# Attention into a feed-forward pair on one core: where the last softmax sums, scalings and roundings are put

## The chip, the cores and the metric

One core of one Trainium2 chip. The metric is device time in microseconds of one execution, the median of several. The kernel before: 574.27 us (three runs, 572.66 to 574.66).

## What is computed

Attention with capped scores (2 batches, 12 heads, 448 positions, head size 64), its output x (896 x 768) through two feed-forward layers, all in float32:

```python
scores = cap * np.tanh(q @ k.T / np.sqrt(64) / cap)
attn = np.exp(scores - max) ; attn /= attn.sum(-1) + 1e-09
x = (attn @ v) laid out as (2 * 448, 12 * 64)
x = (s * relu(x @ w_in) ** 2 + b) @ w_out        # 768 -> 2048 -> 768
h = x @ w2_in
out = (h * clip(h + 3, 0, 6) / 6) @ w2_out       # 768 -> 2048 -> 768
```

## The kernel before

All matrices are held transposed: channels on partitions, 448 positions of one batch on the free axis.

**Attention** goes over 12 pairs of heads (`P = 12`; pairs 0 to 5 are batch 0, pairs 6 to 11 batch 1). A pair's 448 keys are three chunks of 128 and a rest of 64; the rests of two neighbouring pairs form one mixed unit, so two pairs make 7 units (`U = 7`, `N = 42` in all). A unit goes through `scores` (PE, L221 and L225, into PSUM tile `ps`), `tanh` and `exps` (ACT, L229 and L234, tile `t`), `attend` (PE, L244 and L247, adding into the pair's PSUM tile `pav`) and `add_up` (DVE, L256 and L259, adding the exponentials into `acc`). The order is written out by hand: one loop over steps `n` (L358) emits each engine's work, `attend` and `scores` for two units at each even step, and a table `plan` adds the rest at given steps.

The softmax sums of two pairs are made by PE with a matrix of ones: `total` (L266, over `acc`) and `total_rest` (L274, over the mixed unit) write PSUM tile `pz`, of which there is one buffer (`ps_z`, one bank). DVE takes the reciprocal (L276, into `rz`), and DMAs on SP's queue write it to DRAM (L280) and read it back spread over partitions (L282, tile `rb`). `take` (DVE, L300) copies a pair's `pav` to SBUF as `xu`; `finish_x` (DVE) multiplies it by `rb` (L306) and splits it into a rounded part `xh` (L307) and the remainder `xl` (L308). The last two pairs, 10 and 11, do without DRAM: `total_pair` (PE, L289 and L292, also into `pz`; reciprocal L295) gives sums that are already spread.

**The feed-forward part** (`ffn`) works from weights in chunks of 128 x 768. They come as 64-bit numbers and are joined and split in stages: `fetch` (DMA, tile `raw`), `rescale` (DVE L66 or ACT L68), `join` (DVE L80, L82, L84), `upper` (the rounded part `whi`, DVE or ACT, L93), `lower` (the remainder `wlo`, DVE L99). Each product takes three matmuls, `wlo` by `xh`, `whi` by `xl`, `whi` by `xh` (L104). It opens with the first three chunks (`FIRST = 3`, made ready during attention by the table `early`) against batch 0, 54 matmuls into three PSUM tiles `pf`, then against batch 1, 54 more. `pf` has four buffers, which take the banks of `ps` once attention's scores are done. Matmuls of batch 0 (nine a step) begin at step `N - 1 = 41`, between the last steps of attention; those of batch 1 read pair 6's x first and pair 11's last. After batch 0 come the ReLUs (ACT, L110), squares (L114) and `gh`, `gl` (L121, L128), and beside batch 1 chunk 3 is joined and split.

The steps that matter at the end are these:

```python
for d in range(P // 2 - 1):
    at_step(U * d + 11, total, d)
    at_step(U * d + 12, total_rest, d)
    for o in range(2):
        at_step(U * d + 17 + o, finish_x, 2 * d + o)
for p in range(P):
    at_step(U * (p // 2) + 6 + 3 * (p % 2), take, p)
at_step(N - 1, total_pair, P - 2)
at_step(N + 1, finish_x, P - 2)
at_step(N + 2, total_pair, P - 1)
at_step(N + 4, finish_x, P - 1)
```

Of the kernel before, what the change touches and what calls it, by code (L numbers as in the profile page):

```python
# [7 lines left out]
F32 = mybir.dt.float32  # L8
# [7 lines left out]
B, H, S, D = 2, 12, 448, 64  # L16
# [13 lines left out]
def attention_moe_moe(ctx: ExitStack, tc: tile.TileContext, qk, v, cap, w1i, w1o, s, b, w2i, w2o, out):  # L30
    nc = tc.nc
# [12 lines left out]
    x = [[act.tile([128, KD, S], F32R, name=f"x{p}{bi}") for p in ("h", "l")] for bi in range(B)]  # L44
# [9 lines left out]
    def fetch(i):  # L54
        if i < len(chunks):
            src, k0, k1 = chunks[i]
            raws[i] = wp.tile([128, CH * 128, 2], U32, name="raw", tag="raw")
            nc.sync.dma_start(raws[i][:, :(k1 - k0) * 128, :], src[:, k0:k1, :].bitcast(U32).rearrange("p k (m t) -> p (k m) t", t=2))
# [102 lines left out]
    def psum():  # L161
        return ps_f.tile([128, 512], F32, name="pf")
# [28 lines left out]
    at = tc.alloc_tile_pool(name="at", bufs=3)  # L191
    dram = ctx.enter_context(tc.tile_pool(name="dram", bufs=2, space=bass.MemoryType.DRAM))
    ps_v = tc.alloc_tile_pool(name="ps_v", bufs=3, space=PSUM)
    ps_z = tc.alloc_tile_pool(name="ps_z", bufs=1, space=PSUM)
    ps_s = tc.alloc_tile_pool(name="ps_s", bufs=2, space=PSUM)
    P = B * H // 2
    units = [u for d in range(P // 2) for u in [(2 * d, c) for c in range(NC)] + [(2 * d, None)] + [(2 * d + 1, c) for c in range(NC)]]
    N, U = len(units), 2 * NC + 1
    raw_qk, u_ps, u_t, acc, mix, pav, xu, sums, rz, rb = {}, {}, {}, {}, {}, {}, {}, {}, {}, {}
# [5 lines left out]
    def load(p):  # L205
        bi, hp = divmod(p, H // 2)
        raw_qk[p] = at.tile([128, 2, S], F32, name="rqk", bufs=4)
        if p == 0:
            nc.scalar.dma_start(raw_qk[p][:, 1, :], qk[bi, hp, :, 1, :])
            nc.sync.dma_start(raw_qk[p][:, 0, :], qk[bi, hp, :, 0, :])  # L210
        else:
            nc.sync.dma_start(raw_qk[p], qk[bi, hp])

    def scores(n):

        p, c = units[n]
        ps = u_ps[n] = ps_s.tile([128, 2, 512], F32, name="ps")
        for j in range(2):
            rows = (top, end)[j]
            if c is not None:  # L220
                nc.tensor.matmul(ps[:, j, :S], raw_qk[p][rows, 1, c * 128:(c + 1) * 128], raw_qk[p][rows, 0, :], start=True, stop=True)  # L221
        if c is None:
            for o, j, keys, col in MIXED:
                rows = (top, end)[j]
                nc.tensor.matmul(ps[keys, col, :S], raw_qk[p + o][rows, 1, NC * 128:], raw_qk[p + o][rows, 0, :], start=True, stop=True)  # L225

    def tanh(n):
        u_t[n] = at.tile([128, 2, S], F32, name="t", bufs=8)
        nc.scalar.activation(u_t[n], u_ps.pop(n)[:, :, :S], AF.Tanh, scale=icap_r)  # L229

    def exps(n):


        nc.scalar.activation(u_t[n], u_t[n], AF.Exp, scale=cap_r)  # L234

    def attend(n):
        p, c = units[n]
        bi, d = divmod(p // 2, H // 4)
        new = p + 1 if c is None else p if c == 0 and p % 2 == 0 else None
        if new is not None:  # L240
            pav[new] = ps_v.tile([128, 512], F32, name="pav")
        if c is None:
            for o, j, keys, col in MIXED:
                nc.tensor.matmul(pav[p + o][(top, end)[j], :S], va[bi][keys, d, 4 * NC + col, :], u_t[n][keys, col, :], start=o == 1, stop=o == 0)  # L244
            return
        for j in range(2):
            nc.tensor.matmul(pav[p][(top, end)[j], :S], va[bi][:, d, (2 * (p % 2) + j) * NC + c, :], u_t[n][:, j, :],  # L247
                             start=(p % 2 == 0 and c == 0), stop=(p % 2 == 1 and c == NC - 1))
# [35 lines left out]

    def total_pair(p):

        z = ps_z.tile([128, 512], F32, name="pz")
        for j in range(2):
            nc.tensor.matmul(z[(top, end)[j], :S], ones, acc[p][:, j, :], start=True, stop=False)  # L289
        for o, j, keys, col in MIXED:  # L290
            if o == p % 2:
                nc.tensor.matmul(z[(top, end)[j], :S], ones[keys, :], mix[p // 2][keys, col, :], start=False, stop=True)  # L292
        del acc[p]
        rb[p] = at.tile([128, S], F32, name="rz", bufs=2)
        nc.vector.reciprocal(rb[p], z[:, :S])  # L295

    def take(p):

        xu[p] = at.tile([128, S], F32, name="xu", bufs=6)
        nc.vector.tensor_copy(xu[p], pav.pop(p)[:, :S])  # L300

    def finish_x(p):
        bi, hp = divmod(p, H // 2)
        hi, lo = (t[:, hp, :] for t in x[bi])
        xf = xu.pop(p)
        nc.vector.tensor_mul(xf, xf, rb.pop(p))  # L306
        nc.vector.tensor_copy(hi, xf)  # L307
        nc.vector.tensor_sub(lo, xf, hi.bitcast(F32))  # L308

    with tc.manual_schedule():  # L310
        nc.scalar.dma_start(capt, cap)
        load(0)
        nc.sync.dma_start(va[0][:, 0], v[0][:, 0])
        load(1)
        load(2)
        nc.sync.dma_start(va[0][:, 1:], v[0][:, 1:])
        load(3)
        for i in range(3):
            fetch(i)
        nc.sync.dma_start(st, s.to_broadcast([128, 1]))  # L320
        nc.sync.dma_start(bt, b.to_broadcast([128, 1]))
        nc.sync.dma_start(va[1], v[1])
        nc.vector.memset(zeros, 0.0)
        nc.gpsimd.memset(ones, 1.0)
        nc.scalar.activation(three, zeros[:, :1], AF.Tanh)
        warm = ps_z.tile([128, 512], F32, name="pz")
        for columns in WARM:
            nc.tensor.matmul(warm[:, :columns], zeros[:, :128], zeros[:, :columns], start=True, stop=True)
        nc.vector.reciprocal(icap, capt)
        nc.vector.tensor_scalar(icap, icap, SCALE, None, op0=ALU.mult)  # L330
        cap_r, icap_r = (nc.scalar.alloc_register(n) for n in ("cap_r", "icap_r"))
        nc.scalar.reg_load(cap_r, capt.bitcast(I32))
        nc.scalar.reg_load(icap_r, icap.bitcast(I32))
        nc.vector.memset(three, 3.0)
        early = {}
        for i in range(FIRST):
            for j, step in enumerate(((rescale, i, True), (join, i, 0), (join, i, 1), (join, i, 2), (upper, i, True), (lower, i))):
                early[6 + 6 * i + j] = [step]
        early[38] = [(rescale, FIRST)]

        plan = {}
        at_step = lambda n, what, *args: plan.setdefault(n, []).append((what, args))
        for d in range(P // 2 - 1):
            at_step(U * d + 11, total, d)
            at_step(U * d + 12, total_rest, d)
            for o in range(2):
                at_step(U * d + 17 + o, finish_x, 2 * d + o)
        for p in range(P):
            at_step(U * (p // 2) + 6 + 3 * (p % 2), take, p)
        at_step(N - 1, total_pair, P - 2)  # L350
        at_step(N + 1, finish_x, P - 2)
        at_step(N + 2, total_pair, P - 1)
        at_step(N + 4, finish_x, P - 1)
        for p in range(4, P):
            at_step(U * (p // 2 - 2) + 2 + 3 * (p % 2), load, p)
        fill, ps_f = None, None
        has = lambda n: 0 <= n < N
        for n in range(-2, N + 5):  # L358
            if n % 2 == 0 and has(n - 1):
                attend(n - 2)  # L360
                attend(n - 1)
            if n % 2 == 0 and has(n + 2):
                scores(n + 2)
                scores(n + 3)
            if n == N - 1:
                ps_s.release()
                ps_f = tc.alloc_tile_pool(name="ps_f", bufs=4, space=PSUM)
                fill = ffn()
            if n >= N - 1:
                for _ in range(3):  # L370
                    next(fill)
            if has(n):
                exps(n)
            if has(n + 1):
                tanh(n + 1)
            if n % 2 == 0 and has(n - 1):
                add_up(n - 2)
                add_up(n - 1)
            for what, args in plan.get(n, ()):
                what(*args)  # L380
            for step, *args in early.get(n, ()):
                step(*args)
        at.release()
        gp = ctx.enter_context(tc.tile_pool(name="gp", bufs=1))
        for f in range(KF):
            for bi in range(B):
                if (bi, f) not in g:
                    g[bi, f] = [gp.tile([128, S], F32R, name=f"g{p}{bi}{f}") for p in ("h", "l")]
        for _ in fill:
            pass  # L390
        for p in (ps_f, ps_z, ps_v):
            p.release()
# [40 lines left out]
```

## Time and profile before

| | |
|---|---|
| median of three runs | 574.27 us (572.66 to 574.66) |
| profiled execution | 573.65 us, span 571.9 us (first to last instruction) |
| PE busy | 561.4 us, 98% |
| DVE busy | 381.6 us, 67% |
| ACT busy | 257.0 us, 45% |
| chain that ended last | PE 86% (L104 alone 80%), DVE 9%, DMA 3% |
| PE in the 40 slices | `8999997999999999999999999999999999999997` |
| TensorE clock in the 40 slices | `9999998999999999999999999999999999999999` |

A digit of the last two lines is the busy share, or the granted clock, of one fortieth of the span in tenths (9 is 90% or more). The seventh slice, 85.8 to 100.1 us, is where attention ends. In the rows below, a matmul of attention (float32) shows as two instructions, one of the feed-forward part as one; PE rows are read best by their starts, since the ends are modelled and overlap.

### The profile page before, as it was taken

The page shows a single profiled execution, that of the slowest core. Times are in us where ns is not written, and L with a number is a line of the kernel's source. Part 1 is how long each engine was busy: PE and PEld are TensorE (multiplying, and loading weights), DVE is VectorE, ACT ScalarE, POOL GpSimd, SP SyncE. Part 2 cuts the span into 40 slices and gives each one's busy share as a digit, 9 for nine tenths or more (in the row PEclk, how much of TensorE's full clock was granted, in tenths as well). Part 3 has the DMA queues.
Part 4 walks back from the last instruction along what each step waited for, and adds up shares of the span by engine and source line. Part 5 has one row for each costly group of instructions (what it writes and reads, how often), then busy time and mean ns, then how long its engine had stood idle before and what let it go on. Part 6 is the DMA issues. An engine that isn't in the chain of part 4 may idle for free.

```text
span 571.9 us, 6988 instructions
## 1 busy us (share of the span) xinstructions
PE 561.4 (98%) x2790; PEld 460.1 (80%) x2790; DVE 381.6 (67%) x533; ACT 257.0 (45%) x368; POOL 0.4 (0%) x5
## 2 busy tenths in 40 slices
PE   8999997999999999999999999999999999999997
PEld 3223232789999999999999999999999999999996
DVE  2659987899877778446545648888888854554420
ACT  5998892155555554222322334555555522321210
POOL 0000000000000000000000000000000000000000
PEclk9999998999999999999999999999999999999999
DMA  8713421033333324234224323323332345443100
GB/s 344 286 43 126 148 66 61 3 111 110 112 111 112 111 92 135 88 128 122 84 91 146 122 100 111 104 102 103 100 102 89 120 146 156 132 124 122 59 33 33
DMA packets 14987, 64.13 MB, mean 112 GB/s; under 512 B 2006, under 2 KB 3818, under 8 KB 14826
## 3 DMA queue, kind: packets, MB, share of 16 engines
q1 hardware_dynamic: 14808, 63.45, 33.5%
q8 instruction: 22, 0.36, 0.3%
q10 hardware_dynamic: 146, 0.23, 0.1%
q14 instruction: 11, 0.09, 0.1%
HBM read 60.88 MB, written 2.79 MB: 111 GB/s over the span
## 4 chain that ended last, share of the span: by engine, by line
PE 86%; DVE 9%; DMA 3%; issue 1%; ACT 1%; SPq 0%; ACTq 0%; DVEq 0%
PE pf L104 80%; DVE rz L276 3%; PE ps L221 2%; PE pav L247 2%; DMA rb<-rows 1%; DVE xu L306 1%; DVE xl L308 1%; DMA rqk<-in_qk 1%; DVE xh L307 1%; DVE acc L259 1%; DVE acc L256 1%; DMA rows<-rz 1%; PE pz L292 0%; DVE xu L300 0%; PE pz L289 0%
## 5 line engine op out<-in xcount | busy, mean ns | idle before, releaser
L104 PE MATMUL pf<-xl,whi 128*128 128x448 f32 x384 | 140.5, 366 | 0.3 <-DVE xl L308 0.2
L104 PE MATMUL pf<-xh,wlo 128*128 128x448 f32 x384 | 140.7, 366 | 0.0
L104 PE MATMUL pf<-gh,wlo 128*128 128x448 f32 x384 | 140.3, 365 | 0.0
L104 PE MATMUL pf<-gh,whi 128*128 128x448 f32 x384 | 140.3, 365 | 0.0
L104 PE MATMUL pf<-xh,whi 128*128 128x448 f32 x384 | 140.3, 365 | 0.0
L104 PE MATMUL pf<-gl,whi 128*128 128x448 f32 x384 | 140.3, 365 | 0.0
L93 ACT CAST whi<-w 128x768 fp32r<-128x768 f32 (+1 forms) x65 | 51.7, 796 | 166.8 <-PE pf L104 96.9
L99 DVE TENSOR_TENSOR wlo<-w,whi 128x768 fp32r<-128x768 f32 (+1 forms) x68 | 61.7, 907 | 83.7 <-ACT whi L93 83.7
L104 PEld LDWEIGHTS pf<-xh,wlo 128*128 128x128 f32 x384 | 72.2, 188 | 8.1 <-issue 1.4
L104 PEld LDWEIGHTS pf<-xl,whi 128*128 128x128 f32 x384 | 72.1, 188 | 6.6 <-DVE xl L308 0.9
L104 PEld LDWEIGHTS pf<-gh,wlo 128*128 128x128 f32 x384 | 72.2, 188 | 5.7
L104 PEld LDWEIGHTS pf<-gh,whi 128*128 128x128 f32 x384 | 72.2, 188 | 5.7
L104 PEld LDWEIGHTS pf<-xh,whi 128*128 128x128 f32 x384 | 72.2, 188 | 5.7
L104 PEld LDWEIGHTS pf<-gl,whi 128*128 128x128 f32 x384 | 72.2, 188 | 5.7
L84 DVE SCALAR_TENSOR_TENSOR w<-raw,w 128x768 uint32<-128x768 uint32 (+1 forms) x68 | 61.9, 911 | 2.3
L82 DVE SCALAR_TENSOR_TENSOR w<-raw,w 128x768 uint32<-128x768 uint32 (+1 forms) x68 | 62.0, 911 | 2.2
L68 ACT ACTIVATE raw<-raw 128x768 f32<-128x768 f32 (+1 forms) x65 | 56.2, 864 | 0.0
L229 ACT ACTIVATE t<-ps 128x896 f32<-128x896 f32 x42 | 37.9, 902 | 9.9 <-PE ps L221 9.7
L234 ACT ACTIVATE t<-t 128x896 f32<-128x896 f32 x42 | 39.9, 950 | 1.3
L110 ACT ACTIVATE h<-pf 128x448 f32<-128x448 f32 x32 | 16.9, 541 | 44.4 <-PE pf L104 44.4
L80 DVE TENSOR_SCALAR w<-raw 128x768 uint32<-128x768 uint32 (+1 forms) x68 | 35.9, 528 | 0.0
L221 PE MATMUL ps<-rqk 64*128 64x448 f32 x144 | 34.0, 578 | 0.6 <-DMA rqk<-in_qk 0.4
(50 smaller groups left out, 339.9 us busy)
## 6 DMA issues: line engine op xcount, KB each, us to landing
raw<-in_w1i SPq DMA_DIRECT2D x16, 768.0 KB, 4.4
raw<-in_w2i SPq DMA_DIRECT2D x16, 768.0 KB, 4.2
raw<-in_w1o SPq DMA_DIRECT2D x12, 768.0 KB, 4.5
raw<-in_w2o SPq DMA_DIRECT2D x12, 768.0 KB, 4.5
rqk<-in_qk SPq DMA_DIRECT2D x11, 448.0 KB, 7.1
raw<-in_w1o SPq DMA_DIRECT2D x6, 512.0 KB, 3.9
raw<-in_w2o SPq DMA_DIRECT2D x6, 512.0 KB
out<-y SPq DMA_DIRECT2D x12, 224.0 KB, 2.0
```

Source lines behind the costliest of these rows:

```text
L68: nc.scalar.activation(up, up, AF.Copy, scale=2.0**-112)
L80: nc.vector.tensor_scalar(bits, up, 3, None, op0=ALU.logical_shift_left)
L82: nc.vector.scalar_tensor_tensor(out=bits, in0=up, scalar=0x80000000, in1=bits, op0=ALU.bitwise_and, op1=ALU.bitwise_or)
L84: nc.vector.scalar_tensor_tensor(out=bits, in0=low, scalar=29, in1=bits, op0=ALU.logical_shift_right, op1=ALU.bitwise_or)
L93: (nc.vector.tensor_copy if dve else nc.scalar.copy)(ready[i][0][:, :n], whole[i][:, :n])
L99: nc.vector.tensor_sub(lo[:, :n], whole.pop(i)[:, :n], hi[:, :n].bitcast(F32))
L104: nc.tensor.matmul(ps[:, :S], w[a][:, sl], rhs[r], start=(k == 0 and i == 0), stop=(k == n_k - 1 and i == 2))
L110: nc.scalar.activation(t, ps[:, :S], AF.Relu, **({"bias": three} if layer else {}))
L221: nc.tensor.matmul(ps[:, j, :S], raw_qk[p][rows, 1, c * 128:(c + 1) * 128], raw_qk[p][rows, 0, :], start=True, stop=True)
L229: nc.scalar.activation(u_t[n], u_ps.pop(n)[:, :, :S], AF.Tanh, scale=icap_r)
L234: nc.scalar.activation(u_t[n], u_t[n], AF.Exp, scale=cap_r)
L276: nc.vector.reciprocal(rz, z[:, :S])
```

## The change

Sums: the sums of pair 10 go to a `pf` tile and one step later (step 42, behind `attend` of the last two units and nine more feed-forward matmuls); all `total` and `total_rest` are one step earlier. Scaling: pairs 10 and 11 are no longer copied by `take`; the multiplication reads `pav` in PSUM. Rounding: `finish_x` is split into `scale_x` and `rest_x`, and the rounded parts of pairs 8 to 11 are made by ACT. Weights: of the three early chunks, 1 and 2 are rescaled and rounded by ACT, and their stages lie at other steps.

```diff
     def total_pair(p):
-        z = ps_z.tile([128, 512], F32, name="pz")
+        z = psum() if p % 2 == 0 else ps_z.tile([128, 512], F32, name="pz")
...
+    def scale_x(p, engine=nc.vector.tensor_copy):
+        bi, hp = divmod(p, H // 2)
+        last = p >= P - 2
+        xf = xu[p] = at.tile([128, S], F32, name="xu", bufs=6) if last else xu[p]
+        nc.vector.tensor_mul(xf, pav.pop(p)[:, :S] if last else xf, rb.pop(p))
+        engine(x[bi][0][:, hp, :], xf)
+
+    def rest_x(p):
+        bi, hp = divmod(p, H // 2)
+        nc.vector.tensor_sub(x[bi][1][:, hp, :], xu.pop(p), x[bi][0][:, hp, :].bitcast(F32))
+
     def finish_x(p):
-        bi, hp = divmod(p, H // 2)
-        hi, lo = (t[:, hp, :] for t in x[bi])
-        xf = xu.pop(p)
-        nc.vector.tensor_mul(xf, xf, rb.pop(p))
-        nc.vector.tensor_copy(hi, xf)
-        nc.vector.tensor_sub(lo, xf, hi.bitcast(F32))
+        scale_x(p)
+        rest_x(p)
...
         for i in range(FIRST):
-            for j, step in enumerate(((rescale, i, True), (join, i, 0), (join, i, 1), (join, i, 2), (upper, i, True), (lower, i))):
-                early[6 + 6 * i + j] = [step]
+            for j, step in enumerate(((rescale, i, i == 0), (join, i, 0), (join, i, 1), (join, i, 2), (upper, i, i == 0), (lower, i))):
+                early.setdefault(((6, 7, 8, 9, 10, 11), (12, 13, 14, 15, 20, 21), (20, 21, 22, 23, 28, 29))[i][j], []).append(step)
...
         for d in range(P // 2 - 1):
-            at_step(U * d + 11, total, d)
-            at_step(U * d + 12, total_rest, d)
-            for o in range(2):
+            at_step(U * d + 10, total, d)
+            at_step(U * d + 11, total_rest, d)
+            for o in range(2 if 2 * d < P - 4 else 0):
                 at_step(U * d + 17 + o, finish_x, 2 * d + o)
-        for p in range(P):
+        for p in range(P - 2):
             at_step(U * (p // 2) + 6 + 3 * (p % 2), take, p)
-        at_step(N - 1, total_pair, P - 2)
-        at_step(N + 1, finish_x, P - 2)
+        at_step(N, total_pair, P - 2)
+        at_step(N + 2, scale_x, P - 2, nc.scalar.copy)
         at_step(N + 2, total_pair, P - 1)
-        at_step(N + 4, finish_x, P - 1)
+        at_step(N + 2, rest_x, P - 2)
+        for o in (4, 3):
+            at_step(N + 3, scale_x, P - o, nc.scalar.copy)
+        at_step(N + 4, scale_x, P - 1, nc.scalar.copy)
+        for o in (4, 3, 1):
+            at_step(N + 4, rest_x, P - o)
```

How the instructions then stand, at three places. **PE, end of attention** (names: `pz` the old tile of sums, `pf` a feed-forward tile, `pav` the attention output of a pair, `xh`/`xl` the two parts of x, `whi`/`wlo` of the weights). Before, the rows around the sums of pair 10:

```order
L104 MATMUL pf<-xl_75,whi 128x448
L104 MATMUL pf<-xh_74,whi 128x448
L289 MATMUL pz<-acc,ones 64x448 x2
L292 MATMUL pz<-t,ones 64x448 x2
L247 MATMUL pav<-t,va_99 64x448 x4
L104 MATMUL pf<-xh_74,wlo 128x448
```

With the change, from the end of the first nine feed-forward matmuls:

```order
L247 MATMUL pav<-t,va_99 64x448 x4
L104 MATMUL pf<-xh_74,wlo 128x448
L104 MATMUL pf<-xl_75,whi 128x448
L104 MATMUL pf<-xh_74,whi 128x448
L104 MATMUL pf<-xh_74,wlo 128x448
L104 MATMUL pf<-xl_75,whi 128x448
L104 MATMUL pf<-xh_74,whi 128x448
L104 MATMUL pf<-xh_74,wlo 128x448
L104 MATMUL pf<-xl_75,whi 128x448
L104 MATMUL pf<-xh_74,whi 128x448
L289 MATMUL pf<-acc,ones 64x448 x2
L292 MATMUL pf<-t,ones 64x448 x2
```

The sums of pair 10 stand behind the last `attend` and nine more matmuls, and write `pf`. **DVE, the last x** (`rz` a reciprocal, `rb` one that came back from DRAM, `xu` a pair's unrounded x). Before, from the copy of pair 11's `pav` on:

```order
L300 COPY xu<-pav 128x448
L295 RECIPROCAL rz<-pz 128x448
L306 TENSOR_TENSOR xu<-xu,rb 128x448
L307 CAST xh_76<-xu 128x448
L308 TENSOR_TENSOR xl_77<-xu,xh_76 128x448
L306 TENSOR_TENSOR xu<-xu,rb 128x448
L307 CAST xh_76<-xu 128x448
L308 TENSOR_TENSOR xl_77<-xu,xh_76 128x448
L306 TENSOR_TENSOR xu<-xu,rz 128x448
L307 CAST xh_76<-xu 128x448
L308 TENSOR_TENSOR xl_77<-xu,xh_76 128x448
```

With the change, from the reciprocal of pair 10 on:

```order
L295 RECIPROCAL rz<-pf 128x448
L306 TENSOR_TENSOR xu<-pav,rz 128x448
L295 RECIPROCAL rz<-pz 128x448
L311 TENSOR_TENSOR xl_77<-xu,xh_76 128x448
L306 TENSOR_TENSOR xu<-xu,rb 128x448 x2
L306 TENSOR_TENSOR xu<-pav,rz 128x448
L311 TENSOR_TENSOR xl_77<-xu,xh_76 128x448 x3
L114 SCALAR_TENSOR_TENSOR h<-h,st 128x448 x3
```

The casts have left DVE, and the three multiplications (pairs 8, 9, 11) stand ahead of the three remainders. **ACT, behind the last exponential.** Before:

```order
L234 ACTIVATE t<-t 128x896
L110 ACTIVATE h<-pf 128x448 x3
L68 ACTIVATE raw<-raw 128x768
L121 ACTIVATE gh_78<-h,bt 128x448
L121 ACTIVATE gh_80<-h,bt 128x448
```

With the change:

```order
L234 ACTIVATE t<-t 128x896
L307 CAST xh_76<-xu 128x448 x4
L110 ACTIVATE h<-pf 128x448 x3
L68 ACTIVATE raw<-raw 128x768
L121 ACTIVATE gh_78<-h,bt 128x448
```

The four casts stand ahead of batch 0's ReLUs.

## Rows read from the trace of the kernel before

**Rows 1.** Who waited for whom, PE: us in total, times, longest.
```profile
PE pz L289 <- DVE rz L276: 3.4, 1, 3.4
...
PE pz L266 <- DVE acc L259: 0.5, 1, 0.5
...
PE pf L104 <- DVE xl L308: 0.2, 1, 0.2
```
**Rows 2.** Timeline of PE, 82 to 124 us: start, length, instruction, count, idle before.
```profile
82.45 1.73 PE L247 MATMUL pav<-t,va 128*64 128x448 f32 x8
84.10 1.77 PE L221 MATMUL ps<-rqk 64*128 64x448 f32 x8
...
89.40 0.48 PE L104 MATMUL pf<-xh,wlo 128*128 128x448 f32 x1
...
91.15 0.37 PE L104 MATMUL pf<-xh,whi 128*128 128x448 f32 x1
94.95 1.24 PE L289 MATMUL pz<-acc,ones 128*64 128x448 f32 x4 [3.43 <-DVE rz L276]
...
100.00 0.47 PE L104 MATMUL pf<-xh,wlo 128*128 128x448 f32 x1
...
105.37 0.37 PE L104 MATMUL pf<-xh,whi 128*128 128x448 f32 x1
105.67 0.97 PE L289 MATMUL pz<-acc,ones 128*64 128x448 f32 x4
...
107.47 0.47 PE L104 MATMUL pf<-xh,wlo 128*128 128x448 f32 x1
...
111.22 0.37 PE L104 MATMUL pf<-xh,wlo 128*128 128x448 f32 x1
...
113.79 0.47 PE L104 MATMUL pf<-xl,whi 128*128 128x448 f32 x1 [0.19 <-DVE xl L308]
...
115.72 0.36 PE L104 MATMUL pf<-xh,whi 128*128 128x448 f32 x1
...
123.21 0.37 PE L104 MATMUL pf<-xh,wlo 128*128 128x448 f32 x1
```
**Rows 3.** Busy time by stretch: us, PE, PEld, DVE, ACT, POOL, granted clock, DMA.
```profile
96.00:98.00 2.00, 2.00 (x8) 0.48 (x8) 0.07 (x1) 0.00 (x0) 0.00 (x0) 0.50 0.01 4
...
100.00:102.00 2.00, 2.00 (x12) 1.87 (x11) 1.90 (x3) 0.00 (x0) 0.00 (x0) 1.00 0.12 36
```
**Rows 4.** Timeline of DVE, 79 to 122 us.
```profile
79.30 2.95 DVE L276 RECIPROCAL rz<-pz 128x448 f32<-128x448 f32 x1
...
88.69 0.63 DVE L306 TENSOR_TENSOR xu<-xu,rb 128x448 f32<-128x448 f32 x1 [1.24 <-DMA rb<-rows]
...
91.95 2.95 DVE L276 RECIPROCAL rz<-pz 128x448 f32<-128x448 f32 x1
...
107.59 2.96 DVE L295 RECIPROCAL rz<-pz 128x448 f32<-128x448 f32 x1 [2.40 <-PE pz L292]
110.46 0.56 DVE L306 TENSOR_TENSOR xu<-xu,rb 128x448 f32<-128x448 f32 x1
...
111.48 0.63 DVE L308 TENSOR_TENSOR xl<-xu,xh 128x448 fp32r<-128x448 f32 x1
112.03 0.62 DVE L306 TENSOR_TENSOR xu<-xu,rb 128x448 f32<-128x448 f32 x1
...
114.73 0.63 DVE L308 TENSOR_TENSOR xl<-xu,xh 128x448 fp32r<-128x448 f32 x1
...
121.31 0.95 DVE L99 TENSOR_TENSOR wlo<-w,whi 128x768 fp32r<-128x768 f32 x1
```
**Rows 5.** Who waited for whom, ACT, 30 to 90 us.
```profile
ACT t L229 <- PE ps L221: 5.5, 6, 1.6
```
**Rows 6.** Groups by line and shape, 125 to 570 us: busy, mean ns of one.
```profile
L68 ACT ACTIVATE raw<-raw 128x768 f32<-128x768 f32 x50 | 45.4, 907 | 0.0
L93 ACT CAST whi<-w 128x768 fp32r<-128x768 f32 x52 | 43.5, 837 | 154.6 <-PE pf L104 96.9 <-DVE w L84 57.7
...
L117 DVE TENSOR_TENSOR h<-pf,h 128x448 f32<-128x448 f32 x32 | 20.0, 625 | 1.1
...
L123 ACT CAST gh<-h 128x448 fp32r<-128x448 f32 x32 | 16.5, 567 | 0.1
```

## The prediction, made before the changed kernel's time was known

> **What bounds the kernel now.** I read the page first: PE is busy for 561.4 of 571.9 us and carries 86% of the chain that ended last, so a gain has to come out of the 10.5 us in which PE stood still, or out of work that PE did slowly. The list of PE's waits says where: the largest is 3.4 us, once, at the sums of a last pair, which wait for a reciprocal on DVE [rows 1]. The reader should see that nearly everything else on the list is tenths.
>
> Next the timeline of PE at that place [rows 2]. Nine feed-forward matmuls run from 89.40, the last starts at 91.15. Then PE stands until 94.95, when pair 10's sums start. The tile `pz` has one buffer; it still holds the sums of pairs 8 and 9, and their reciprocal runs on DVE only from 91.95 for 2.95 us [rows 4]. Behind the sums in PE's order stand the last `attend` and every further matmul, so the whole engine waits. The wait has a tail: sums and `attend` take from 94.95 to 100.00, 5.05 us, though their pieces take 1.80 (105.67 to 107.47) and 1.65 (82.45 to 84.10) elsewhere [rows 2]. [...]
>
> At the other end of this stretch, batch 1's first matmuls wait in pieces for the `xl` of the last pairs, 113.13 to 115.72 [rows 2], while DVE still splits x until 115.36 [rows 4]. From the 72nd feed-forward matmul (115.72) PE runs without a wait on the list.
>
> **Part by part, from the first feed-forward matmul (89.40) to the 72nd (115.72): 26.32 us now.**
>
> *Sums of pair 10 in `pf`.* Nothing is in the way of that tile: three `pf` tiles hold batch 0's results, this is the fourth. The work of PE in its new order is, from [rows 2]: nine matmuls, 1.75 for eight starts and 0.30 to the next group (105.37 to 105.67), 2.05; `attend` 1.65; nine more, 2.05; sums of pair 10, 1.80; 18 matmuls 3.85 (107.47 to 111.22, and 0.10 for the change of group); sums of pair 11, 1.80; 18 matmuls 3.75; 17 starts at 3.75/18, 3.54. Sum 20.49, so 26.32 holds 5.83 us too much. It splits into 3.50 of standing (91.45 to 94.95), 1.60 of half clock (5.05 less 3.45) and 0.73 of waits for `xl`. The first two go: **5.10 us**. They go even if DVE were as late as before: pair 11's sums, which still need `pz`, start at 89.40 + 2.05 + 1.65 + 2.05 + 1.80 + 3.85 = 100.80, and the reciprocal that holds it ends at 94.90 [rows 4].
>
> *What is late next: x of pairs 8 to 11.* The sums of pair 11 start at 100.80, their reciprocal 1.92 later (105.67 to 107.59 before), at 102.72. It holds DVE for 2.87 (107.59 to 110.46); then come, 0.55 apart (111.48 to 112.03), the remainder of 10, the products of 8, 9 and 11, the remainders of 8, 9 and 11 [rows 4]. The remainder of 8 starts at 105.59 + 4 x 0.55 = 107.79 and ends at 108.42. PE begins batch 1 at 100.80 + 1.80 + 3.75 = 106.35 and needs that remainder seven starts later, at 107.81. So it waits some 0.65 us, and with a restart 0.75: as much as the 0.73 before, a term of nothing. The remainders of 9 and 11 end at 108.97 and 109.52, at about or before their use.
>
> *Casts on ACT.* ACT has nothing to do there; a cast of this shape takes 0.57 us [rows 6]. Pair 8's product ends near 106.75, its cast by 107.4, before DVE comes to its remainder; pair 11's product ends at 107.87 and its cast at 108.45, before 108.89, where its remainder is due. On DVE the chain from the reciprocal of pair 11 to the last `xl` shrinks from 7.77 (107.59 to 115.36) to 6.8. No further term.
>
> *Products read from PSUM.* Two copies fall away on DVE; `pav` is held longer, but no later pair asks for it. A product with one operand in PSUM takes 625 ns (L117), from SBUF 0.62 us (L306) [rows 4, 6]: no term.
> [...]
>
> *Early chunks on ACT.* ACT gains two rescalings and two roundings, 2 x 0.91 + 2 x 0.84 = 3.5 us [rows 6], between its exponentials. Their cover is the 5.5 us, in six pieces, in which ACT waits for PE from 30 to 90 us [rows 5]. DVE is relieved by as many. Bounds: nothing lost, or all 3.5 us; I take nothing, since the added pieces lie at four steps and PE has a whole unit in stock at each, and keep a part of it for the range.
>
> *Sums one step earlier.* In front of `attend` they do the same work on PE. The 0.5 us in which the sums waited for `acc` [rows 1] may go, as DVE is less behind; against it, scores behind such a group come one group, 0.9 us, later, and ACT with them. Bounds 0.5 gained and 0.9 lost; I take nothing. On SP one fetch of weights changes place with one load of q and k; that chunk is used only in the feed-forward part. The reciprocals' DMAs keep their places among the loads.
>
> **Sum.** The profiled execution took 573.65 us: 571.9 of span and 1.75 around it. Less 5.10 that is 568.55, forecast **568.6 us**. The profiled execution lies 0.6 under the median of 574.27, within the runs' spread.
>
> **Rivals.**
>
> *ACT becomes a bound in attention.* For it: from 30 us on, PE's scores need the tanh of two units before, and the added work comes in lumps of up to 1.7 us. Against it: 5.5 us of ACT's idle time against 3.5 of work. With all of it on PE's path: 568.55 + 3.5 = 572.0, no change to speak of.
>
> *The wait moves to chunk 3.* The first matmul that needs it stands 37 starts behind the 72nd, at 123.21 before, and its `wlo` ended at 122.26 [rows 2, 4], only 1 us ahead. If that chain (ReLU, squares, joins) came no earlier, PE would win 1.0: 572.6. Against it: the chain hangs on the last `xl`: from its start, 114.73, to 122.26 are 7.53 us. With the last remainder at 108.89 it ends at 116.4; PE, 5.1 earlier, needs it at 118.1.
>
> *ReLUs behind the casts: slower.* On ACT batch 0's ReLUs now queue behind four casts, and pair 11's cast queues behind DVE's products of 8 and 9, which wait for `rb` to come back from DRAM. PE's 73rd matmul, near 110.8, writes a `pf` tile that a ReLU must have read; it should be free by 109.0 (108.45 and one ReLU). If `rb` came late, PE would stand again, and a stand as long as the old one brings the half clock: 3.5 us of it with 1.6 of clock eat the whole gain. That is the point from which it decides: the last cast 5.3 us later than worked out. To be over 0.5% slower takes 2.9 more: some 577. For it: DVE did wait for `rb` at 88.69. Against it: that was 6.4 us behind the end of its reciprocal (82.25); even from 94.90, as late as before, `rb` would be there at 101.3, and it is first needed at 106.1 [rows 4].
>
> **How the numbers follow.** A measurement of this kernel can tell about 0.5% (2.9 us) from no change, so faster means under 571.4. The forecast has 0.87, ACT as a bound 0.06, chunk 3 0.04 (both no change), the ReLUs 0.03. Range: downwards both waits that I left in (0.5 and 0.7) give 567.4, and the runs spread by some tenths more: 567.0. Upwards the 0.9 of the earlier sums, part of ACT's 3.5 and the spread: 571.0.
>
> **What would show it.** Right: PE's wait at L289 for L276 is gone, the granted clock stays at 1.00 from 86 to 102 us, the stretch from the first to the 72nd feed-forward matmul takes about 21.2 us, and the first of them still starts near 89.4. The steps are wrong, each by itself, if the first L104 starts after 90.5 (ACT), if the wait for `xl` exceeds 1.5 us, if PE waits for `wlo` of chunk 3 or for a ReLU, or if PE waits at L289 for anything. A time above 571.4 would make the prediction wrong.

## The result, and the profile after

The changed kernel took 567.23 and 567.28 us, where the kernel before takes 574.27: ratio 0.9885, 95% interval 0.9842 to 0.9928. That is 7.0 us less; the forecast was 5.7 less (568.6 us), with a range from 567.0 to 571.0. Two more executions of it took 576.31 and 578.0 us; single ones of the kernel before (583.2 to 583.5 us) and of e5, e7 and e10 below also took about 9 us more, and the comparisons leave those out.

The profiled execution took 567.23 us with a span of 565.4, so the span lost 6.5 us (571.9 before). The page's first part and the start of its fourth:

```profile
PE 558.6 (99%) x2790; PEld 459.2 (81%) x2790; DVE 376.8 (67%) x523; ACT 261.1 (46%) x376; POOL 0.4 (0%) x5
...
PE 94%; ACT 3%; issue 1%; DMA 1%; DVE 0%; ACTq 0%
```

DVE stood in 9% of the chain that ended last, and is now out of it. Who PE waited for, the whole list:

```profile
PE pz L335 <- DVE zeros L330: 1.4, 1, 1.4
PE ps L225 <- ACT t L229: 0.8, 1, 0.8
PE ps L221 <- ACT t L229: 0.4, 2, 0.3
PE ps L221 <- DMA rqk<-in_qk: 0.3, 1, 0.3
PE pf L104 <- DVE xl L311: 0.3, 1, 0.3
```

Of [rows 1] the wait of 3.4 us (L289 for L276) and the one of 0.5 us (L266 for `acc`) are gone; the wait for `xl` stands at 0.3. PE at the end of attention, as in [rows 2]:

```profile
88.21 0.47 PE L104 MATMUL pf<-xh,wlo 128*128 128x448 f32 x1
...
90.23 1.72 PE L247 MATMUL pav<-t,va 128*64 128x448 f32 x8
...
93.90 0.97 PE L289 MATMUL pf<-acc,ones 128*64 128x448 f32 x4
...
95.70 0.47 PE L104 MATMUL pf<-xh,wlo 128*128 128x448 f32 x1
...
99.60 0.97 PE L289 MATMUL pz<-acc,ones 128*64 128x448 f32 x4
...
105.22 0.37 PE L104 MATMUL pf<-xh,wlo 128*128 128x448 f32 x1
...
107.14 0.47 PE L104 MATMUL pf<-xl,whi 128*128 128x448 f32 x1 [0.32 <-DVE xl L311]
...
109.27 0.36 PE L104 MATMUL pf<-xh,whi 128*128 128x448 f32 x1
```

Both groups of sums start without a wait, and from the first feed-forward matmul (88.21) to the 72nd (109.27) are 21.06 us, for 26.32 before. The view by stretches, columns as in [rows 3], shows a granted clock of 1.00 where it had been 0.50:

```profile
96.00:98.00 2.00, 2.00 (x11) 1.83 (x10) 2.00 (x1) 0.00 (x0) 0.00 (x0) 1.00 0.00 0
```

DVE in the same stretch, as in [rows 4]: it now waits for PE ahead of both reciprocals of the last pairs; ahead of the first of these sums PE used to wait for DVE.

```profile
87.15 2.95 DVE L276 RECIPROCAL rz<-pz 128x448 f32<-128x448 f32 x1
...
95.82 2.96 DVE L295 RECIPROCAL rz<-pf 128x448 f32<-128x448 f32 x1 [3.57 <-PE pf L292]
...
101.52 2.96 DVE L295 RECIPROCAL rz<-pz 128x448 f32<-128x448 f32 x1 [2.09 <-PE pz L292]
...
106.47 1.69 DVE L311 TENSOR_TENSOR xl<-xu,xh 128x448 fp32r<-128x448 f32 x3
...
114.12 0.95 DVE L99 TENSOR_TENSOR wlo<-w,whi 128x768 fp32r<-128x768 f32 x1
```

So 5.26 us of the 6.5 come from where the forecast put them. The other 1.2 lie ahead of it: the first feed-forward matmul starts at 88.21 in place of 89.40, which the forecast held unchanged. To find them the span is cut at three starts that every trace shows: the scores of a mixed unit near 51 us (L225), the first and the 72nd feed-forward matmul. The kernels e1, e2 and so on are those of the next section.

| profiled execution of | to L225 | to 1st L104 | to 72nd L104 | to the end | span |
|---|---|---|---|---|---|
| before | 51.42 | 37.98 | 26.32 | 456.2 | 571.9 |
| the change | 50.85 | 37.36 | 21.06 | 456.1 | 565.4 |
| e1_tile_back | 50.85 | 37.36 | 21.06 | 456.1 | 565.4 |
| e2_tile_only | 51.29 | 37.98 | 21.28 | 456.2 | 566.7 |
| e3_place_only | 51.70 | 37.98 | 21.55 | 456.2 | 567.4 |
| e4_early_back | 51.04 | 36.52 | 21.10 | 456.1 | 564.8 |
| e5_sums_late | 50.85 | 36.51 | 21.11 | 456.1 | 564.6 |
| e6_dve_casts | 51.62 | 37.35 | 22.35 | 456.2 | 567.5 |
| e7_early_spread | 51.06 | 36.52 | 21.10 | 465.1 | 573.8 |
| e9_best | 50.89 | 36.52 | 20.52 | 465.1 | 573.0 |
| e10_wait_back | 51.16 | 36.51 | 21.26 | 456.2 | 565.1 |
| e11_wait_short | 51.63 | 36.51 | 20.72 | 456.1 | 565.0 |
| e12_after_no_wait | 50.82 | 37.35 | 20.51 | 465.1 | 573.8 |

The first column differs by up to 0.8 us between kernels whose programs are the same up to there (the change shows 50.85 and e6, which differs in the last casts alone, 51.62). The 0.57 us between the kernel before and the change are of that kind: the first scores of a mixed unit start at 10.12 us before and at 9.53 with the change, ahead of everything that was changed, and from there to the ones near 51 us are 41.30 and 41.32. The second and third columns repeat to some hundredths wherever the program does; so does the fourth, but for the 9 us more of e7, e9 and e12, of which more below.

### The profile page after: what moved, and what is told of

It is laid out like the page before. It is cut to its first block, busy times and chain, and to the rows that moved or that the text cites. A ratio compares the mean times of both kernels' runs of the same rounds, so it can differ in the third digit from the quotient of the medians.

```text
span 565.4 us, 6987 instructions
## 1 busy us (share of the span) xinstructions
PE 558.6 (99%) x2790; PEld 459.2 (81%) x2790; DVE 376.8 (67%) x523; ACT 261.1 (46%) x376; POOL 0.4 (0%) x5
## 4 chain that ended last, share of the span: by engine, by line
PE 94%; ACT 3%; issue 1%; DMA 1%; DVE 0%; ACTq 0%
PE pf L104 82%; PE ps L221 5%; PE pav L247 4%; ACT t L229 2%; PE pav L244 1%; ACT t L234 1%; PE pz L266 1%; DMA rqk<-in_qk 1%; PE ps L225 1%; PE pz L274 1%; DVE xu L306 0%; DVE xl L311 0%; PE pz L292 0%; PE pf L289 0%; PE pz L289 0%
## 5 line engine op out<-in xcount | busy, mean ns | idle before, releaser
L104 PE MATMUL pf<-xh,wlo 128*128 128x448 f32 x384 | 140.7, 366 | 0.0
L104 PE MATMUL pf<-xl,whi 128*128 128x448 f32 x384 | 140.4, 366 | 0.3 <-DVE xl L311 0.3
L104 PE MATMUL pf<-xh,whi 128*128 128x448 f32 x384 | 140.3, 365 | 0.0
L104 PE MATMUL pf<-gl,whi 128*128 128x448 f32 x384 | 140.2, 365 | 0.0
L104 PE MATMUL pf<-gh,whi 128*128 128x448 f32 x384 | 140.2, 365 | 0.0
L104 PE MATMUL pf<-gh,wlo 128*128 128x448 f32 x384 | 140.2, 365 | 0.0
L93 ACT CAST whi<-w 128x768 fp32r<-128x768 f32 (+1 forms) x67 | 53.4, 797 | 166.3 <-PE pf L104 96.9
L99 DVE TENSOR_TENSOR wlo<-w,whi 128x768 fp32r<-128x768 f32 (+1 forms) x68 | 61.7, 907 | 83.7 <-ACT whi L93 83.7
L104 PEld LDWEIGHTS pf<-xh,wlo 128*128 128x128 f32 x384 | 72.1, 188 | 8.5 <-issue 2.1
L104 PEld LDWEIGHTS pf<-xl,whi 128*128 128x128 f32 x384 | 72.1, 188 | 6.4 <-DVE xl L311 0.7
L104 PEld LDWEIGHTS pf<-xh,whi 128*128 128x128 f32 x384 | 72.1, 188 | 5.7
L104 PEld LDWEIGHTS pf<-gh,wlo 128*128 128x128 f32 x384 | 72.1, 188 | 5.7
L104 PEld LDWEIGHTS pf<-gh,whi 128*128 128x128 f32 x384 | 72.1, 188 | 5.7
L104 PEld LDWEIGHTS pf<-gl,whi 128*128 128x128 f32 x384 | 72.1, 188 | 5.7
L68 ACT ACTIVATE raw<-raw 128x768 f32<-128x768 f32 (+1 forms) x67 | 58.1, 867 | 0.0
L110 ACT ACTIVATE h<-pf,three 128x448 f32<-128x448 f32 x32 | 20.2, 632 | 27.9 <-PE pf L104 27.9
```

The source lines that it names most:

```text
L68: nc.scalar.activation(up, up, AF.Copy, scale=2.0**-112)
L93: (nc.vector.tensor_copy if dve else nc.scalar.copy)(ready[i][0][:, :n], whole[i][:, :n])
L99: nc.vector.tensor_sub(lo[:, :n], whole.pop(i)[:, :n], hi[:, :n].bitcast(F32))
L104: nc.tensor.matmul(ps[:, :S], w[a][:, sl], rhs[r], start=(k == 0 and i == 0), stop=(k == n_k - 1 and i == 2))
L110: nc.scalar.activation(t, ps[:, :S], AF.Relu, **({"bias": three} if layer else {}))
```

## The experiments

**e1 and e2, e3: which half of the edit on the sums of pair 10 takes the wait away?** Theory A: the free `pf` tile. Theory B: the later place alone. e1 is the changed kernel with the old tile:

```diff
-        z = psum() if p % 2 == 0 else ps_z.tile([128, 512], F32, name="pz")
+        z = ps_z.tile([128, 512], F32, name="pz")
```

> The changed kernel with the sums of pair 10 back in the one-buffer tile pz, at their new place. Theory A (the other PSUM tile took the wait away): the sums wait for the reciprocal of pairs 8 and 9 again, PE stands for some 3 us and the half clock follows, about 572 us. Theory B (the place behind attend and nine more matmuls took it away, and the tile is not needed): with the change the reciprocal ended at 90.0 us and the sums started at 93.9, so no wait, first to 72nd feed-forward matmul 21.1 us, time as the changed kernel, 567.2 within 0.5.

Measured: 567.08 to 567.61 us, ratio 0.9888 [0.9860, 0.9915]. The timeline is that of the change, with `pz` where it has `pf`:

```profile
93.89 0.97 PE L289 MATMUL pz<-acc,ones 128*64 128x448 f32 x4
94.80 0.97 PE L292 MATMUL pz<-t,ones 64*64 64x448 f32 x4
```

No wait: in the later place the old tile has long been read (its reciprocal ends at 90.10 in the change's rows above). With the other edits in, the tile is worth nothing. e2 and e3 put one half each into the kernel before. e2:

```diff
-        z = ps_z.tile([128, 512], F32, name="pz")
+        z = psum() if p % 2 == 0 else ps_z.tile([128, 512], F32, name="pz")
```

> The kernel before with the sums of pair 10 in a pf tile, at their old place, nothing else. Both theories: no wait for L276 at these sums. PE goes on at 91.45; granted clock 1.00 throughout. DVE's chain is as before, so the x of pairs 9 and 11 comes late and PE waits up to 1.5 us for it: first to 72nd feed-forward matmul 21 to 22 us against 26.3, about 569 us.

e3:

```diff
-        at_step(N - 1, total_pair, P - 2)
-        at_step(N + 1, finish_x, P - 2)
+        at_step(N, total_pair, P - 2)
+        at_step(N + 2, finish_x, P - 2)
```

> The kernel before with the sums of pair 10 still in pz but one step later, behind attend and nine more matmuls, and its x one step later; nothing else. Theory A: the wait stays, some 3.4 us with the half clock behind it, 573.5 us. Theory B: the sums come to their turn at 95.15, the reciprocal that holds pz ended at 94.9, so no wait above 0.3 us; first to 72nd feed-forward matmul 21 to 22 us, about 569 us.

Measured: e2 568.44 to 569.22 us, ratio 0.9914 [0.9886, 0.9942]; e3 568.42 to 569.15 us, ratio 0.9912 [0.9884, 0.9940]. Either half alone takes 26.32 to 21.28 or 21.55, all but 0.2 to 0.5 us of what the whole change brings there. Neither touches the stretch before it: 37.98, as before.

**e4, e5, e7: where did attention win, and what did it pay?** Theory C: the early chunks on ACT cost time and the earlier sums of all pairs bring it. e4 is the change with the early chunks as they were, on DVE at steps 6 to 23:

```diff
-            for j, step in enumerate(((rescale, i, i == 0), (join, i, 0), (join, i, 1), (join, i, 2), (upper, i, i == 0), (lower, i))):
-                early.setdefault(((6, 7, 8, 9, 10, 11), (12, 13, 14, 15, 20, 21), (20, 21, 22, 23, 28, 29))[i][j], []).append(step)
+            for j, step in enumerate(((rescale, i, True), (join, i, 0), (join, i, 1), (join, i, 2), (upper, i, True), (lower, i))):
+                early[6 + 6 * i + j] = [step]
```

> The changed kernel with the three early weight chunks as in the kernel before (all of it on DVE, at the old steps). Theory C (the early chunks cost: ACT's four added pieces made PE wait or go slowly for 0.8 us at 52, 54.6 and 67 us): these three go, scores at those places take 0.91, 1.71 and 1.71 us; first feed-forward matmul up to 0.8 us earlier unless DVE is late. Theory D (they gain: they leave DVE ahead, which took away the wait of the sums for acc at 56.7 to 59.0 us, 1.4 us): the sums of pairs 4 and 5 wait for acc again and take up to 2.3 us in place of 0.9. Time 566.5 by C, 568.0 by D.

Measured: 566.57 to 566.92 us, ratio 0.9878 [0.9851, 0.9906]; attention's stretch 36.52. e5 takes the other part back, the sums one step earlier:

```diff
-            at_step(U * d + 10, total, d)
-            at_step(U * d + 11, total_rest, d)
+            at_step(U * d + 11, total, d)
+            at_step(U * d + 12, total_rest, d)
```

> The changed kernel with all sums of pairs 0 to 9 one step later again, as before. Theory E (the earlier sums took away the wait of the sums of pairs 4 and 5 for acc): they again take 2.3 us in place of 0.9, first feed-forward matmul 1.4 us later, about 568.6. Theory F (the lighter DVE of the early chunks is enough by itself): they take 0.9; and, as scores 20, 21, 34 and 35 are no longer pushed back by 0.9, ACT loses less: the scores at 54.6 and 67 us take 1.8 in place of 1.9 and 2.1, about 566.8.

Measured: 566.41 and 566.98 us, no interval; the stretch 36.51. So Theory C is only half right, and of e5's two Theory F holds: each part alone wins 1.46 us (37.98 less 36.52), and the two together win 0.62. They do the same thing twice and then collide. What each wins shows in the timeline at the sums of pairs 4 and 5. Before:

```profile
56.70 0.95 PE L266 MATMUL pz<-acc,ones 128*32 128x448 f32 x4
58.12 0.95 PE L266 MATMUL pz<-acc,ones 128*32 128x448 f32 x4 [0.48 <-DVE acc L259]
59.00 0.98 PE L244 MATMUL pav<-t,va 64*64 64x448 f32 x8
```

e5, with DVE relieved and the sums in their old place:

```profile
56.07 0.96 PE L266 MATMUL pz<-acc,ones 128*32 128x448 f32 x8
56.96 0.98 PE L244 MATMUL pav<-t,va 64*64 64x448 f32 x8
```

The group takes 2.30 us where a wait splits it and 0.89 where none does: 1.41 us for a wait that the list gives as 0.5. What was paid shows at the scores. The change:

```profile
50.85 0.98 PE L225 MATMUL ps<-rqk 64*64 64x448 f32 x8
52.02 1.02 PE L221 MATMUL ps<-rqk 64*128 64x448 f32 x4 [0.19 <-ACT t L229]
...
54.63 2.00 PE L221 MATMUL ps<-rqk 64*128 64x448 f32 x8
56.55 0.96 PE L266 MATMUL pz<-acc,ones 128*32 128x448 f32 x8
...
67.02 2.14 PE L221 MATMUL ps<-rqk 64*128 64x448 f32 x8
69.09 0.96 PE L266 MATMUL pz<-acc,ones 128*32 128x448 f32 x8
```

e4, the same places:

```profile
51.04 0.98 PE L225 MATMUL ps<-rqk 64*64 64x448 f32 x8
51.95 1.02 PE L221 MATMUL ps<-rqk 64*128 64x448 f32 x4
...
54.56 1.77 PE L221 MATMUL ps<-rqk 64*128 64x448 f32 x8
56.27 0.96 PE L266 MATMUL pz<-acc,ones 128*32 128x448 f32 x8
...
66.73 1.77 PE L221 MATMUL ps<-rqk 64*128 64x448 f32 x8
68.44 0.96 PE L266 MATMUL pz<-acc,ones 128*32 128x448 f32 x8
```

Start to start the three groups take 1.17, 1.92 and 2.07 us in the change, 0.91, 1.71 and 1.71 in e4: 0.26, 0.21 and 0.36, together 0.83 of the 0.84 us that lie between the two stretches. Only 0.19 of it is listed as a wait. But in the change the later scores of each group start 0.05 us after the end of a tanh (tanh to 51.97, 55.55 and 68.08 us, scores from 52.02, 55.60 and 68.14), so at all three places PE waits for ACT; in e4 the tanh ahead of the second place ended at 55.03, 0.39 us before the scores. On ACT a rounding and a rescaling of weights stand back to back between a tanh and its exponential, some microseconds ahead of the first of these places:

```profile
46.92 0.82 ACT L93 CAST whi<-w 128x768 fp32r<-128x768 f32 x1
47.64 0.93 ACT L68 ACTIVATE raw<-raw 128x768 f32<-128x768 f32 x1
```

A second rounding, at 63.82 us, stands ahead of the third place. e7 makes both roundings two steps sooner, so that the two pieces of step 20 stand apart, and leaves the earlier sums in:

```diff
-                early.setdefault(((6, 7, 8, 9, 10, 11), (12, 13, 14, 15, 20, 21), (20, 21, 22, 23, 28, 29))[i][j], []).append(step)
+                early.setdefault(((6, 7, 8, 9, 10, 11), (12, 13, 14, 15, 18, 19), (20, 21, 22, 23, 26, 27))[i][j], []).append(step)
```

> The changed kernel with the roundings of early chunks 1 and 2 on ACT two steps sooner (18 and 26 in place of 20 and 28), remainders likewise: the two pieces at step 20 no longer stand in one lump, and the second rounding falls before ACT's longest idle time (1.1 us near 60). If the lump and the place cost the 0.8 us in attention, it goes down to 0.2 to 0.4: scores at 67 us 1.71 again, about 566.7. If any added work on ACT costs its share of PE, the time stays at 567.2.

Measured: ratio 0.9887 [0.9868, 0.9905], 566.47 to 568.24 us; in its trace (of an execution that took 575.53 us, so that only this part is compared) attention's stretch is 36.52, from 51.06 to 87.58. So neither the pieces on ACT nor the earlier sums cost anything by themselves: e5 has the same pair of pieces back to back, e7 the same sums, and neither loses. The two together do. As e7 moves both roundings, the runs don't tell which place hangs on which of them.

**e6: do the casts on ACT matter?** The change with the four casts back on DVE:

```diff
-        at_step(N + 2, scale_x, P - 2, nc.scalar.copy)
+        at_step(N + 2, scale_x, P - 2)
...
-            at_step(N + 3, scale_x, P - o, nc.scalar.copy)
-        at_step(N + 4, scale_x, P - 1, nc.scalar.copy)
+            at_step(N + 3, scale_x, P - o)
+        at_step(N + 4, scale_x, P - 1)
```

> The changed kernel with the casts of pairs 8 to 11 on DVE again, in the new order (all casts ahead of the remainders). If the casts' move to ACT matters as worked out, the remainder of pair 8 comes three casts later on DVE (3 x 0.39 and the gaps between dependent instructions, some 1.6 us): PE waits 2.0 us in place of 0.5 for xl and the first to 72nd matmul take 22.7 us against 21.1; about 568.8. If it does not matter, 567.2.

Measured: 568.71 to 569.47 us, ratio 0.9921 [0.9905, 0.9937]. The wait for `xl` grows from 0.3 to 1.6 us:

```profile
109.19 0.47 PE L104 MATMUL pf<-xl,whi 128*128 128x448 f32 x1 [1.60 <-DVE xl L311]
```

The stretch to the 72nd matmul is 1.29 us longer (22.35); another 0.77 of this execution lies ahead of 51 us, where the program is the same. The casts' move is worth the 1.29.

**e9: the version that should have been best.** e4, with the products of pairs 8 and 9 ahead of pair 11's reciprocal and the remainders in the order 8, 9, 10, 11, so that no `xl` is late:

```diff
-        at_step(N + 2, scale_x, P - 2, nc.scalar.copy)
+        for o in (2, 4, 3):
+            at_step(N + 2, scale_x, P - o, nc.scalar.copy)
         at_step(N + 2, total_pair, P - 1)
-        at_step(N + 2, rest_x, P - 2)
-        for o in (4, 3):
-            at_step(N + 3, scale_x, P - o, nc.scalar.copy)
         at_step(N + 4, scale_x, P - 1, nc.scalar.copy)
-        for o in (4, 3, 1):
+        for o in (4, 3, 2, 1):
             at_step(N + 4, rest_x, P - o)
```

> The changed kernel with the early chunks as before (as in the run without them, 566.7) and with the products of pairs 8 and 9 ahead of pair 11's reciprocal, in the 2 us in which DVE stands idle. Pair 8's remainder then comes 1 us sooner on DVE, before PE asks for it: no wait for xl, first to 72nd matmul 20.5 us in place of 21.1, about 566.1. If the wait for xl was not on the path, 566.7.

Measured: 574.79 to 575.7 us in nine runs, ratio 1.0024 [1.0013, 1.0034]: a miss by 9 us. The wait is gone and the stretch to the 72nd matmul is the shortest yet, 20.52; all of the loss lies behind it, 465.1 us for 456.1, where the matmuls and the granted clock (1.00) are the same. Over the 2232 intervals from the 72nd L104 to the last the starts tell where it goes. The last six of one kind, in the timeline of the change (shortest, median and longest in ns, first and last start):

```profile
L104 PE MATMUL pf<-gh,whi x6: 362/365/369, 558.6 to 561.6; 128*128 128x448 f32 x6
```

The same in e9:

```profile
L104 PE MATMUL pf<-gh,whi x6: 367/368/368, 566.1 to 569.2; 128*128 128x448 f32 x6
```

From 109.27 to 561.6 the change starts one every 202.7 ns, from 107.93 to 569.2 e9 one every 206.7: 4.0 ns more, and by 2232 that is 8.9 us. The length shown has changed as well, from 362 to 369 ns to 368 for nearly all.

**e10, e11, e12: is it the missing wait?** In the changed kernel, too, the matmuls ahead of the wait for `xl` start 0.207 us apart, and those behind it 0.203. Theory G: a break in PE's stream lets it take up another cadence, and without a break it keeps the slow one. Rival: the order of the work on DVE and ACT, or the chunks of e4, do it. e10 is e9 with one order changed, which brings the wait back:

```diff
-        for o in (4, 3, 2, 1):
+        for o in (3, 2, 1, 4):
             at_step(N + 4, rest_x, P - o)
```

> The kernel without a wait for xl (574.8 us, feed-forward matmuls 206.7 ns start to start to the end), with one order of four numbers changed: the remainders of the last four pairs go 9, 10, 11, 8 in place of 8, 9, 10, 11. The remainder of pair 8 then ends some 1.6 us later on VectorE (about 106.5 for 104.8 us), and the matmul that reads it, at 105.9, waits about 0.5 us. Theory G (after a break in the stream of matmuls the engine takes up a new cadence; here it should be 202.7 ns as in the other kernels with such a wait): about 2230 intervals of 4.0 ns less, 8.9 us, and the wait more: 566.2 to 566.8 us. Rival (the slow cadence comes from the products standing ahead, that is from what VectorE and ScalarE do there, and the wait has nothing to do with it): 575.2 to 575.5 us. Rival (a wait only shifts work): the same.

e11 is e9 with another order, meant to leave no wait or hardly one:

```diff
-        for o in (4, 3, 2, 1):
+        for o in (3, 2, 4, 1):
             at_step(N + 4, rest_x, P - o)
```

> As the last, but the remainders go 9, 8, 10, 11: that of pair 8 ends at about 105.4 us on VectorE, 0.5 us before the matmul that reads it is due, so that no wait or one under 0.1 us is left. Theory G: no break, so the slow cadence stays and the time is 574.5 to 575.5 us; if a wait of 0.05 us or more does show, the cadence falls to 202.7 ns and the time to 565.9 to 566.4 us. The rival (order of the work on VectorE, whichever order, is harmless) cannot tell it from the kernel with 8, 9, 10, 11.

e12 is the changed kernel with e9's order of products and remainders (e9's edit above) and nothing else:

> The changed kernel with nothing but the last products and remainders put in the order of the kernel without the wait (products of pairs 8 and 9 ahead of the reciprocal of pair 11, remainders 8, 9, 10, 11); the early chunks stay as in the change. Theory G: the wait of 0.32 us for xl is gone, the cadence stays at 206.7 ns, about 8.9 us more and 0.5 less: 575.0 to 576.0 us. Rival (the slow cadence had to do with the early chunks being moved back): 566.6 to 567.0 us.

Measured: e10 566.67 and 566.86 us, with its wait of 0.50 us, and 576.32 and 575.69 in two more executions; no interval. e12 575.58 to 576.82 us in ten runs, ratio 1.0035 [1.0023, 1.0047]: without its wait the change takes 8.5 us more than its 567.23 and 567.28. e11 566.13 to 566.92 us, ratio 0.9866 [0.9846, 0.9886]. Its edit does not do what its expectation says: the numbers 3, 2, 4, 1 put the remainders in the order 9, 10, 8, 11, and not 9, 8, 10, 11. So pair 8's is the third of the four in this row of DVE; it ends at 106.67, and the matmul that reads it starts at 106.72. The break was there, and too short for the list of waits. e11 at this place:

```profile
104.98 2.22 DVE L311 TENSOR_TENSOR xl<-xu,xh 128x448 fp32r<-128x448 f32 x4
...
106.39 0.37 PE L104 MATMUL pf<-xh,wlo 128*128 128x448 f32 x1
106.72 0.47 PE L104 MATMUL pf<-xl,whi 128*128 128x448 f32 x1
107.03 0.36 PE L104 MATMUL pf<-xh,whi 128*128 128x448 f32 x1
107.23 0.37 PE L104 MATMUL pf<-xh,wlo 128*128 128x448 f32 x1
...
108.86 0.36 PE L104 MATMUL pf<-xh,whi 128*128 128x448 f32 x1
```

e12 at the same place, in which one start follows the other:

```profile
106.41 0.37 PE L104 MATMUL pf<-xh,wlo 128*128 128x448 f32 x1
106.62 0.37 PE L104 MATMUL pf<-xl,whi 128*128 128x448 f32 x1
106.82 0.37 PE L104 MATMUL pf<-xh,whi 128*128 128x448 f32 x1
...
108.89 0.37 PE L104 MATMUL pf<-xh,wlo 128*128 128x448 f32 x1
```

One start comes 0.33 us behind the last in place of 0.207, a break of some 0.13 us, and the 2200 matmuls behind it took 9 us less than in e12: from 107.03 to 108.86 e11 has nine intervals of 0.203 us, where e12 has eleven of 0.206 from 106.62 to 108.89. e12 excludes e4's chunks as the cause, e10 and e11 exclude the place of the products. What e9 and e12 have in common, and no other kernel has, is the missing break and the order 8, 9, 10, 11 of the remainders that takes it away. No run has one without the other, so that the break does it is argued and not shown. Nor is a break enough: two of e10's four executions, and two of the change's, took as long as e12's or longer.

By its trace e11 is the best of all: 36.51 and 20.72 are 1.2 us less than the change in these two stretches. The runs show 0.3 to 1.1 us less than the change's 567.23, too little for the intervals to tell apart.

## Why the prediction was right, step by step

- **Sums of pair 10: right.** Forecast 5.10 us (3.50 of standing, 1.60 of half clock), measured 5.26; both parts went, as the missing wait (3.43 us before) and the granted clock of 1.00 in 96 to 98 us (0.50 before) show. The sum of PE's work in the new order, 20.49, is what e12 took without a wait: 20.51. The 0.16 more is nearly all the wait for `xl`, which cost 0.55 (21.06 less 20.51) where 0.73 had been left in. But the free tile, with which the prediction began, was not needed: e1 has none and shows the same trace, while e2 and e3 show that tile and place each suffice.
- **Casts on ACT and `xl`: right.** Forecast: the wait stays about as it was. The remainder of pair 8 began at 106.47, where the forecast has 107.79, or 106.60 counted from the earlier start of L104. e6 shows that the unchanged wait is the casts' doing: with them on DVE it is 1.6 us.
- **Products from PSUM: right.** In the groups of the change, 30 to 125 us, a product from `pav` takes 620 ns and one from `xu` 618:

```profile
L306 DVE TENSOR_TENSOR xu<-xu,rb 128x448 f32<-128x448 f32 x10 | 6.1, 618 | 3.1 <-DMA rb<-rows 3.1
L306 DVE TENSOR_TENSOR xu<-pav,rz 128x448 f32<-128x448 f32 x2 | 1.2, 620 | 0.0
```

- **Sums one step earlier: the step that was mis-sized.** The prediction read the wait for `acc` as 0.5 us at most, and took nothing for it. It was worth 1.41, and the relief of DVE alone would have taken it too (e5). The list of waits gives the idle time; it does not give what a wait does to a group that it splits.
- **Early chunks on ACT: mis-sized, inside the bounds.** Taken as nothing, with 0 to 3.5 us as bounds; beside the earlier sums they cost 0.83, in three pieces, and without them nothing (e5). ACT's idle time behind PE in 30 to 90 us went from 5.5 to 2.8 us [rows 5]. The argument, that a unit in stock covers each piece, failed for the steps that were chosen; two steps sooner the roundings are covered (e7).
- **The first L104 stayed near 89.4: wrong,** by 1.19 us: 0.57 from the first 10 us, by chance, and 0.62 from these last two steps, 1.46 less 0.84. With the 0.16 above that is the 1.3 us by which the forecast was too long.
- **The rivals.** ACT as a bound cost 0.8 and not 3.5. Chunk 3 was ready (L99 at 114.12 for a matmul due 37 starts behind the 72nd, near 116.8), and no ReLU was waited for. The rival that counts most is one that I did not have. The prediction takes everything behind the 72nd matmul as unchanged, without a reason. It was (456.1 us for 456.2), and that was luck: in e12, where every `xl` is ready in time, the same stretch takes 465.1 and the kernel is a little slower than the one before, at 1.0035.

## What to carry over

PE's waits had three prices here: the idle time on the list (3.43 us at pair 10's sums), the half clock that followed that one (granted 0.50, worth 1.60 us; the execution of e6, with a wait of 1.60 us, had a mean granted clock of 1.00), and the matmuls side by side that a wait tears apart (2.30 us for 0.89 at the sums of pairs 4 and 5, with 0.48 on the list). Read all three from start to start in the timeline, against the same group elsewhere. Two edits that cure the same wait need not add up, and can collide (1.46 us each, 0.62 together): try each alone. When a kernel is held by one long stream of matmuls, compare their starts to the nanosecond before and after an edit: here 4.0 ns each came to 8.9 us, where the longest wait left in the change is 1.4.

## What the runs showed of the hardware that was not expected

**Two cadences at one clock.** The same matmul (128 x 128 by 448 columns) is started every 202.7 or every 206.7 ns, both at a granted clock of 1.00 (in 200 to 220 us of the change and of e9). All kernels here run at the longer one, 0.206 or 0.207 us, just ahead of the wait for `xl` or of the place where the others have it (the one before: just ahead of its stand at 91 us). A break as short as some 0.13 us (e11) was followed by the shorter one to the end, and the two kernels without a break took 574.79 us or more in all 19 executions, where 34 of the 42 executions of the change, e1 to e7, e10 and e11 took 569.5 us or less. The break is not all of it: the other eight took 575.5 to 578.0, and e7's trace is of one of them (575.53 us). There the starts behind the wait, after the first, came at 106.83, 107.03, 107.24 and 107.44 us, 0.203 apart in the mean, and from there every 0.207, with no break in sight, 465.1 us behind the 72nd start as in e9 and e12; none of the other seven has a trace. The cadence also changes where no wait is listed: the change runs the first 18 of its feed-forward matmuls at 0.202 and goes over to 0.206 or 0.207 behind the sums of pair 10 (95.70 us). What sets the cadence, and what the break changes, stays open.

**Matmuls side by side.** The sums of two pairs are eight instructions of 32 columns each (128*32 in their row). In the kernel before, at 73.80 us, each of the eight takes 0.54 to 0.56 us by its record, and the eight together 0.96 by the length in their row, 0.89 to the start of the next group: several ran at a time. Where the wait splits them (56.70 us), the four ahead of it take 0.95 and the four behind it 0.95 again: the wait in their middle cost the group once more.
